# A scan-and-FFN kernel on one core: the second pair's output products before the third FFN step, the third pair's loads behind a mask

## The chip, the cores and the metric

The kernel runs on one core of one Trainium2 chip. A core has TensorE (PE in the profile), which multiplies matrices into PSUM; VectorE (DVE), ScalarE (ACT) and GpSimd (POOL) for element work; SyncE (SP), whose queue issues transfers; and 16 DMA engines. The metric is the device time of one execution, in microseconds (us); lower is better.

## The reference

A state-space scan runs over 4 batches of 8 heads, 768 positions, head width 32 and state width 16. Its output, 3072 tokens of width 256, goes through a feed-forward layer (FFN) with 2048 hidden units and a squared relu.

```python
for c in range(nc):                                  # chunks of 32 positions
    L = np.exp(cum[:, :, :, None] - cum[:, :, None, :]) * causal
    M = np.einsum('bhin,bhjn->bhij', Cc, Bc) * L
    y_intra = np.einsum('bhij,bhjd->bhid', M, xc)
    y_inter = np.einsum('bhin,bhnd->bhid', Cc, state) * decay_to_i[:, :, :, None]
    y[:, :, sl] = y_intra + y_inter
    Bx = np.einsum('bhjn,bhjd->bhjnd', Bc, xc) * decay_from_j[:, :, :, None, None]
    state = decay_full[:, :, None, None] * state + np.sum(Bx, axis=2)
x = attn_out.transpose(0, 2, 1, 3).reshape(B * S, H * D)
h = np.maximum(x @ w_in, 0.0)
out = h * h @ w_out
```

The result does not depend on the chunk length; the kernel uses chunks of 128 positions. All inputs and the output are float32 in memory.

## The kernel before

**Pairs.** The tokens are cut into 12 blocks of 256, one for each batch and third of the sequence, called pairs because each holds two chunks of 128 positions. Pair k has number k in the code, from 0: the "second pair" is k = 1, the "third" k = 2. The first four pairs are the first thirds of the four batches and need no earlier state.

**What one pair does.** Its C, B and x are loaded (`ph_load`, L122) into buffers of a pool of three. `prep_c`, `prep_b` and `prep_x` (L148, L164, L180) scale and cast them to bf16: cz, Bb and xs. `ph_tr` (L202) transposes Bb and cz on PE and copies them to bct. `ph_mt` (L220) multiplies them to the matrix M in PSUM, and `ph_mask` (L236) applies the causal mask on DVE, in four quarters q = 0 to 3, into mts. `ph_u` (L242) computes the chunk's contribution U to the state, and `ph_s` (L265) turns it into the state. `ph_y` (L324) computes the output: `y_intra` (L307) has 32 small products of mts and xs that go through the quarters in the order 0, 1, 2, 3, then 8 products with the state; ScalarE copies the sum to T in bf16 (L366).

**The FFN.** A pair's FFN has 8 steps. Step (pair, f) multiplies T with two of the 16 column tiles of w_in (`mm1`, L372, four products "hps"), applies relu on ScalarE into hb, squares on DVE (`square`, L384) and, four steps later, multiplies with two row tiles of w_out (`mm2`, L390, four products "ops"). The PSUM pool for hps has two buffers, so a step can begin only when the relu of the step two before it has read its buffer. `warm` (L473) issues dummy products ("dps").

**What sets the order.** The order of work on each engine is written out by hand (`tc.manual_schedule`, L450); waits between engines follow from the data. After a prologue for pair 0, a loop (L629) goes through the list `steps`: first four steps of pair 0, then four of pair 1, then the rest. At each s it issues `mm1`, then whatever `at(s, ...)` put into `todo`, then a square and an `mm2`. `ph_y(1)` is called at the top of s = 3, ahead of the fourth step's `mm1` and behind the third's. The masks of pair 1 come at s = 0 (q = 0, 1) and at s = 1 (q = 3, then q = 2, both from a bf16 copy mtc that ScalarE makes at s = 0).

**When loads start.** SP issues the loads in program order. With `gate=nc.gpsimd`, GpSimd first writes one element of each destination buffer, and the load waits for that write; so a load cannot start before GpSimd's queue has come to it. The weights are loaded from GpSimd's own queue, cast on the way: w_in in four parts (`load_wi`, L135) and w_out in four (`load_wo`, L140). `late_loads` (L568) holds the last three of them until T of pair 1 exists, by copying one element of it to `touch`. The load of pair 2 stands in the prologue (L552), ahead of w_in tiles 8 to 11 on GpSimd's queue.

Of the kernel before, what the change touches and what calls it, by code (L numbers as in the profile page):

```python
# [16 lines left out]
def _fap(base: bass.AP, offset_elems: int, free_dims):  # L17

    ap0 = list(base.ap)[0]
    return bass.AP(tensor=base.tensor, offset=base.offset + offset_elems,  # L20
                   ap=[list(ap0)] + [list(d) for d in free_dims])


def _dap(base: bass.AP, offset_elems: int, dims):

    return bass.AP(tensor=base.tensor, offset=base.offset + offset_elems,
                   ap=[list(d) for d in dims])
# [3 lines left out]
def kernel(  # L31
# [14 lines left out]
    nc = tc.nc  # L46
# [51 lines left out]
    touch = const.tile([128, 1], FP32, name="touch")  # L98
# [23 lines left out]
    def ph_load(k, order="CBx", eng=None, gate=None):  # L122
        b, j = PAIRS[k]
        t = loaded.setdefault(k, {})
        for what in order:
            src, w = {"B": (B, N), "C": (C, N), "x": (x, D)}[what]
            dst = nat.tile([128, NH, 2 * w], FP32, tag=f"{what}_nat", name=f"{what}_nat{k}")
            if gate is not None:
                gate.memset(dst[:, 0, 0:1], 0.0)
            (eng or nc.sync).dma_start(  # L130
                out=dst, in_=_dap(src, (b * NH * S + j * 256) * w,
                                  [[2 * w, 128], [S * w, NH], [1, 2 * w]]))
            t[what] = dst
# [12 lines left out]
    live = {}  # L146
# [225 lines left out]
    def mm1(blk, fp):  # L372
        hps = ps_h.tile([128, 2, 256], FP32, tag="hps", name=f"hps{blk}_{fp}")
        for i in range(2):
            f = 2 * fp + i
            for g in range(2):
                nc.tensor.matmul(hps[:, i, :], w_in_b[:, g, f * 128:(f + 1) * 128],  # L377
                                 T[blk][:, g].rearrange("p r u t -> p (r u t)"),
                                 start=(g == 0), stop=(g == 1), skip_group_check=True)
        hb = fpool.tile([128, 2, 256], BF16, tag="hb", name=f"hb{blk}_{fp}")  # L380
        nc.scalar.activation(out=hb, in_=hps, func=AF.Relu)  # L381
        hbs[(blk, fp)] = hb

    def square(blk, fp):  # L384
        hb = hbs.pop((blk, fp))
        h2 = hpool.tile([128, 2, 256], BF16, tag="h2", name=f"h2{blk}_{fp}")
        nc.vector.tensor_tensor(out=h2, in0=hb, in1=hb, op=ALU.mult)  # L387
        h2s[(blk, fp)] = h2

    def mm2(blk, fp):  # L390
        if fp == 0:
            t = ps_o.tile([128, 2, 256], FP32, tag="ops", name=f"ops{blk}")
            ops[blk] = [[t[:, 0, :]], [t[:, 1, :]]]
            if blk == NPAIR - 1:
                ops[blk][1] = [ps_s.tile([128, 128], FP32, tag="A", name=f"ops_r1{c}", padded_shape=[128, 1024])
                               for c in range(2)]
            else:
                ops_t[blk] = t
        h2 = h2s.pop((blk, fp))
        for i in range(2):  # L400
            f = 2 * fp + i
            for r in range(2):
                o = ops[blk][r]
                for c in range(len(o)):
                    nc.tensor.matmul(o[c], h2[:, i, r * 128:(r + 1) * 128],  # L405
                                     w_out_b[:, f, c * 128:(c + 1) * 128] if len(o) > 1 else w_out_b[:, f, :],
                                     start=(f == 0 and (r == 0 or blk == NPAIR - 1)), stop=(f == 15),
                                     skip_group_check=True)
        if fp == 7:
            finish_block(blk)  # L410
# [39 lines left out]
    with tc.manual_schedule():  # L450
# [17 lines left out]
        def idle_tile(pool=ps_o, tag="ops"):  # L468
            idle.append(pool.tile([128, 256], FP32, tag=tag, name=f"dps{len(idle)}", padded_shape=[128, 512]))
# [3 lines left out]
        def warm(n, cols=256):  # L473
            for _ in range(n):
                nc.tensor.matmul(idle[-1][:, 0:cols], dum[:, 0:128], dum[:, 0:cols],  # L475
                                 start=True, stop=True, skip_group_check=True)
# [13 lines left out]
        for r in range(2):  # L490
            nc.scalar.copy(out=_fap(C_r, r * 128, [[16, 2], [32, 4], [1, 16]]),
                           in_=_fap(loaded[0]["C"], r * 16, [[128, 2], [32, 4], [1, 16]]))
# [28 lines left out]
        def recip(b0, nb, j):  # L521

            nc.vector.reciprocal(out=_fap(Pinv, b0 * 24 + j, [[96, 2], [3, 8 * nb]]),
                                 in_=_fap(P_sb, b0 * 24 + j, [[96, 2], [3, 8 * nb]]))
# [24 lines left out]
        ph_y(0)  # L549
        ph_tr(1)  # L550
        recip(2, 2, 0)
        ph_load(2, gate=nc.gpsimd)  # L552
        idle_tile()
        warm(3, 128)

# [5 lines left out]
        def at(s, fn, *args):  # L561
            todo.setdefault(max(s, 0), []).append((fn, args))
# [9 lines left out]
            load_wo(12, 16)  # L572

        at(0, load_wi, 8, 12)
        at(3, own_decay)
        at(5, late_loads)
        at(6, lambda: ph_load(3, gate=nc.gpsimd))
# [49 lines left out]
            at(yy, ph_y, k)  # L627
        waiting = []
        for s in range(len(steps) + LAG):  # L629
            if s == 3:  # L630
                ph_y(1)
            if s < len(steps):
                mm1(*steps[s])
                waiting.append(steps[s])
            if 1 <= s < 3:
                warm(3, 128)
            if s == 4:
                waiting[2:4] = []
            if s == 6:
                waiting[2:2] = steps[2:4]  # L640
            for fn, args in todo.pop(s, []):
                fn(*args)
            if 1 <= s < len(steps) + 1:
                square(*steps[s - 1])
            if 4 <= s < len(steps):
                mm2(*waiting.pop(0))
# [31 lines left out]
```

## Time and profile before

| | |
|---|---|
| median of 13 runs | 119.5 us |
| lowest and highest | 118.05 and 123.81 us |
| the profiled execution's own time | 118.05 us |
| its span, first to last instruction | 116.3 us |
| granted TensorE clock | 1.000 |
| busy: PE, weight loads, DVE, ACT, POOL | 94%, 77%, 74%, 66%, 30% |
| moved by DMA | 13.63 MB, mean 117 GB/s |

The profile describes one execution. Its times are microseconds from the first instruction. "SPq" is SP's queue at the moment at which it issues a transfer; "PEld" is the loading of weights into TensorE, which overlaps with products. An entry in brackets at a line of the timeline is the idle time of that engine just before it, and what ended it. "issue" is time in which an engine waited for nothing that the profile shows. In the lists of transfers the last number is the time from issue to landing.

### The profile page before, as it was taken

How to read it: one execution, taken by the hardware profiler on the slowest of the kernel's cores; microseconds unless marked ns; L12 is line 12 of the kernel's file. 1: busy time of each engine (PE TensorE's matmuls, PEld its weight loads, DVE VectorE, ACT ScalarE, POOL GpSimd, SP SyncE). 2: the span in 40 equal slices, each digit the busy share in tenths (PEclk: the TensorE clock that was granted, in tenths of full speed). 3: DMA queues.
4: the chain of work that ended last, by engine and by line, in shares of the span. 5: the costliest groups of instructions: out<-in, count | busy, mean ns of one | idle time of the engine just before them, and what ended most of it. 6: DMA issues, size and time to landing. Idle time of an engine off the chain costs nothing.

```text
span 116.3 us, 4065 instructions
## 1 busy us (share of the span) xinstructions
PE 109.2 (94%) x1672; PEld 89.8 (77%) x1672; DVE 86.4 (74%) x204; ACT 76.3 (66%) x146; POOL 34.3 (30%) x69
## 2 busy tenths in 40 slices
PE   6798889999999999999999999999999999999970
PEld 4575568787787788887887887887887888898960
DVE  6588837699599898895996995986966958744530
ACT  4563877667777666677586675775865965777720
POOL 0099337305894440701333324304300000000000
PEclk9999999999999999999999999999999999999999
DMA  3999999998899908719729939979060020200203
GB/s 90 190 176 154 162 207 189 131 201 136 166 234 178 200 25 163 164 58 175 111 90 169 85 99 204 44 159 185 3 158 8 13 77 6 82 8 0 94 2 90
DMA packets 50019, 13.63 MB, mean 117 GB/s; under 512 B 44304, under 2 KB 49104, under 8 KB 50000
## 3 DMA queue, kind: packets, MB, share of 16 engines
q1 hardware_dynamic: 46400, 10.98, 53.4%
q0 software_dynamic: 3200, 2.10, 13.4%
q10 hardware_dynamic: 400, 0.28, 1.0%
q8 instruction: 13, 0.21, 0.8%
q14 instruction: 6, 0.05, 0.2%
HBM read 10.74 MB, written 3.15 MB: 119 GB/s over the span
## 4 chain that ended last, share of the span: by engine, by line
PE 78%; DMA 10%; DVE 4%; POOL 2%; ACT 1%; issue 1%; ACTq 0%; DVEq 0%; SPq 0%
PE ops L405 33%; PE hps L377 32%; DMA w_in_b<-in_moe_w_in_dram 5%; PE Y L314 3%; DMA C_nat<-in_C_dram 3%; PE mt L227 3%; DMA cf<-const_f 3%; DVE mts L238 2%; PE Y L343 2%; PE U L256 1%; POOL xs L183 1%; POOL bc L152 1%; PE ops_r L405 1%; PE ops L421 1%; PE ops_r L421 1%
## 5 line engine op out<-in xcount | busy, mean ns | idle before, releaser
L381 ACT ACTIVATE hb<-hps 128x512 bf16<-128x512 f32 x96 | 57.6, 600 | 29.9 <-PE hps L377 28.8
L377 PE MATMUL hps<-T,w_in_b 128*128 128x256 bf16 x384 | 57.6, 273 | 0.7 <-DVE bct L217 0.4
L405 PE MATMUL ops<-w_out_b,h 128*128 128x256 bf16 x360 | 55.0, 273 | 0.0
L387 DVE TENSOR_TENSOR h<-hb 128x512 bf16<-128x512 bf16 x96 | 41.9, 460 | 10.7 <-ACT hb L381 10.5
L377 PEld LDWEIGHTS <-w_in_b 128*128 128x128 bf16 x384 | 37.2, 98 | 5.4 <-DMA w_in_b<-in_moe_w_in_dram 0.8
L405 PEld LDWEIGHTS <-h 128*128 128x128 bf16 x376 | 34.5, 98 | 6.3 <-issue 2.0
L238 DVE TENSOR_TENSOR mts<-mt,cb 128x512 bf16<-128x512 f32 x44 | 29.0, 682 | 9.0 <-PE mt L227 9.0
L183 POOL TENSOR_TENSOR xs<-x_nat,Pinv 128x512 bf16<-128x512 f32 x12 | 13.5, 1123 | 12.1 <-DMA x_nat<-in_x_dram 8.5
L152 POOL TENSOR_TENSOR bc<-C_nat,P_sb 128x128 bf16<-128x128 f32 x16 | 6.6, 433 | 21.6 <-DMA C_nat<-in_C_dram 17.8
L475 PE MATMUL dps<-dum 128*128 128x128 bf16 (+1 forms) x58 | 6.8, 264 | 1.1 <-DVE dum L457 1.1
L300 DVE TENSOR_TENSOR S<-z,Pown 128x256 bf16<-128x256 f32 x16 | 7.3, 458 | 0.5
L366 ACT CAST T<-Y 128x512 bf16<-128x512 f32 x11 | 6.4, 585 | 0.5 <-PE Y L347 0.5
L443 ACT COPY osb<-ops 128x512 f32<-128x512 f32 x11 | 6.4, 581 | 0.2 <-PE ops L405 0.2
L475 PEld LDWEIGHTS <-dum 128*128 128x128 bf16 x58 | 4.6, 110 | 2.3 <-DVE dum L457 1.1
L314 PE MATMUL Y<-mts,xs 64*32 64x128 bf16 x384 | 5.2, 219 | 0.2 <-issue 0.2
L227 PE MATMUL mt<-bct 32*64 32x256 bf16 x192 | 5.1, 280 | 0.2 <-DVE bct L515 0.2
L177 POOL CAST bc<-B_nat 128x128 bf16<-128x128 f32 x16 | 5.2, 350 | 0.4 <-DMA B_nat<-in_B_dram 0.4
L314 PEld LDWEIGHTS <-xs 64*32 64x32 bf16 x384 | 3.0, 91 | 1.8 <-issue 0.7
L227 PEld LDWEIGHTS <-bct 32*64 32x64 bf16 x192 | 1.9, 102 | 2.7 <-issue 1.7
L293 DVE SCALAR_TENSOR_TENSOR z<-z,Ptot,U 128x64 f32<-128x64 f32 x12 | 3.2, 266 | 0.4 <-PE U L256 0.3
L141 POOL DMA_DIRECT2D w_out_b<-in_moe_w_out_dram x4 | 3.1, 780 | 0.3 <-issue 0.3
L217 DVE COPY bct<-tr 128x768 bf16<-128x768 bf16 x3 | 1.7, 556 | 2.0 <-PE tr L210 2.0
(72 smaller groups left out, 54.9 us busy)
## 6 DMA issues: line engine op xcount, KB each, us to landing
x_nat<-in_x_dram SPq DMA_DIRECT2D x12, 256.0 KB, 4.4
out_dram<-osb SPq DMA_DIRECT2D x7, 256.0 KB, 2.4
C_nat<-in_C_dram SPq DMA_DIRECT2D x12, 128.0 KB, 3.4
B_nat<-in_B_dram SPq DMA_DIRECT2D x12, 128.0 KB, 3.7
w_in_b<-in_moe_w_in_dram POOLq DMA_DIRECT2D x4, 256.0 KB, 6.0
w_out_b<-in_moe_w_out_dram POOLq DMA_DIRECT2D x4, 256.0 KB, 6.8
out_dram<-osb SPq DMA_DIRECT2D x8, 128.0 KB, 1.8
bct<-bc SPq DMA_TRANSPOSE x8, 4.7
```

Of the source, the lines that this page charges most:

```text
L152: eng.tensor_tensor(out=_fap(bc[k % 3], r * 384 + 128, [[144, 2], [32, 4], [1, 16]]), in0=_fap(loaded[k]["C"], r * 16, [[128, 2], [32, 4], ...
L183: eng.tensor_tensor(out=_fap(xs, 0, [[256, 2], [32, 8], [1, 32]]), in0=_fap(loaded[k]["x"], 0, [[32, 2], [64, 8], [1, 32]]), in1=_fap(Pinv ...
L227: nc.tensor.matmul(mt[q // 2][64 * u:64 * u + 64, q % 2, r, :, :], bct[32 * q:32 * q + 32, r, 0, u * 64:u * 64 + 64], _fap(bct[32 * q:32 * ...
L238: nc.vector.tensor_tensor(out=v["mts"][:, q], in0=v["mt"][q // 2][:, q % 2] if src is None else src, in1=_fap(cb, 128, [[128, 2], [0, 2], ...
L300: nc.vector.tensor_tensor(out=S_n.rearrange("p (g q d) -> p g q d", g=2, q=4), in0=_fap(z, 0, [[32, 2], [0, 4], [1, 32]]), in1=_fap(Pown, ...
L314: nc.tensor.matmul(Y[u][32 * q:32 * q + 32, g, :], v["xs"][64 * u:64 * u + 64, r, h * 32:h * 32 + 32], v["mts"][64 * u:64 * u + 64, q, r, ...
L366: nc.scalar.copy(out=_fap(T[k], 0, [[64, 2], [128, 4], [1, 64]]), in_=_fap(Y[0], 0, [[512, 2], [64, 4], [1, 64]]))
L377: nc.tensor.matmul(hps[:, i, :], w_in_b[:, g, f * 128:(f + 1) * 128], T[blk][:, g].rearrange("p r u t -> p (r u t)"), start=(g == 0), stop ...
L381: nc.scalar.activation(out=hb, in_=hps, func=AF.Relu)
L387: nc.vector.tensor_tensor(out=h2, in0=hb, in1=hb, op=ALU.mult)
L405: nc.tensor.matmul(o[c], h2[:, i, r * 128:(r + 1) * 128], w_out_b[:, f, c * 128:(c + 1) * 128] if len(o) > 1 else w_out_b[:, f, :], start= ...
L475: nc.tensor.matmul(idle[-1][:, 0:cols], dum[:, 0:128], dum[:, 0:cols], start=True, stop=True, skip_group_check=True)
```

## The change

Two things are moved. `ph_y(1)`, the output products of the second pair, is called at s = 2 instead of s = 3, so it stands ahead of the third FFN step's products on PE, and its copy to T ahead of that step's relu on ScalarE. And the third pair's loads leave the prologue: at s = 2 GpSimd first copies one element of quarter 2 of the second pair's masked matrix to `touch`, and only then writes the gates of the three loads. On GpSimd's queue they now stand behind the load of w_in tiles 8 to 11.

```diff
@@ prologue
         ph_y(0)
         ph_tr(1)
         recip(2, 2, 0)
-        ph_load(2, gate=nc.gpsimd)
         idle_tile()
         warm(3, 128)
@@ schedule
         at(0, load_wi, 8, 12)
+
+        def third_loads():
+            nc.gpsimd.tensor_copy(out=touch, in_=live[1]["mts"][:, 2, 0, 0, 0:1])
+            ph_load(2, gate=nc.gpsimd)
+
+        at(2, third_loads)
         at(3, own_decay)
@@ loop
         for s in range(len(steps) + LAG):
-            if s == 3:
+            if s == 2:
                 ph_y(1)
             if s < len(steps):
                 mm1(*steps[s])
```

The number of products and of bytes is the same; GpSimd has one more instruction, the copy to `touch`.

## The prediction

> **What bounds the kernel now.** I read the page's fourth part first (the chain of work that ended last), then that chain in order of time from 12 to 17 us, then the timeline of all engines there, then the transfers.
>
> ```profile
> PE 78%; DMA 10%; DVE 4%; POOL 2%; ACT 1%; issue 1%; ACTq 0%; DVEq 0%; SPq 0%
> ```
>
> TensorE (PE) carries 78% of the chain. The shares do not say where it can be shortened; the order of time does. Columns are start, length, work:
>
> ```profile
> 8.00 5.60 DMA w_in_b<-in_moe_w_in_dram
> 13.60 0.05 issue
> 13.64 0.61 PE hps L377 x4
> 14.25 0.17 PE dps L475 x3
> 14.42 0.34 PE Y L314 x29
> 14.76 0.15 issue
> 14.91 0.23 PE Y L314 x3
> 15.14 0.25 PE Y L347 x8
> 15.39 0.02 issue
> 15.41 0.59 ACT T L366
> 16.01 0.04 issue
> 16.05 0.60 PE hps L377 x4
> ```
>
> Until 16.05 us the start-up is a chain of waits: w_in tiles 4 to 7 land at 13.60, the third FFN step runs, then the second pair's output products (Y), then ScalarE's copy into T, and at 16.05 the fifth step, the first to read that T. From 16.05 on, PE hardly stops: the windows view has it busy 8.55 of the 8.55 us to 24.60. So a shift of the 16.05 goes to the end one for one, and so does any new hole. The change works exactly before this point.
>
> The timeline has what else must be ready (start, length, engine, line, work):
>
> ```profile
> 13.22 0.75 DVE L238 TENSOR_TENSOR mts<-mtc,cb 128x512 bf16<-128x512 bf16 x2
> 13.26 0.25 PE L256 MATMUL U<-xs,Bb 64*32 64x64 bf16 x16 [0.42 <-ACT mtc L587]
> 13.62 0.31 ACT L279 ACTIVATE Sf<-U,Ptot 128x64 bf16<-128x64 f32 x1
> 26.64 0.42 PE L314 MATMUL Y<-mts,xs 64*32 64x128 bf16 x32
> 27.33 0.58 ACT L366 CAST T<-Y 128x512 bf16<-128x512 f32 x1
> ```
>
> The pair's four masks are done at 13.22 + 0.75 = 13.97, its state (Sf) at 13.93. The last two lines are the same product block one pair later: 0.69 from its first product to its T copy.
>
> **Part 1: Y ahead of the third step.** No arithmetic is added or removed: four hps products and three dummy ones change places with 40 Y products; on ScalarE the T copy goes ahead of the third step's relu. What was serial (landing, hps, Y) now overlaps with the masks, so Y starts earlier, yet not at PE's 13.51 (end of U): the third product needs mask slot 2, which the code masks last, at 13.97. Release to start costs 0.06 (T ends 15.99, hps starts 16.05), so Y runs from 14.03 and T could begin at 14.03 + 0.69 = 14.72 and end at 15.30, 0.69 earlier than 15.99.
>
> Most of that is not gained. The fifth step also needs a free hps buffer, and that is freed by the third step's relu, which now stands behind T on ScalarE. The third step follows the state products by 0.22 (15.07 to 15.29 in the trace), so it runs from 14.03 + 0.35 + 0.22 = 14.60 to 15.21; its relu (0.60, row "hb<-hps") goes from 15.25, overlapping T's tail by 0.05 as it does now, to 15.85; the fifth step starts at 15.90. Gain: **0.15 us**. The landing at 13.60 is then off the path, covered until 14.60; with that cover gone it would again be 13.64 plus the block.
>
> The 0.15 of "issue" at 14.76 decides the sign. It is PE's only wait of that name in this kernel: 29 products leave, the 30th does not until 14.91, and nothing is waited for. The page's third part has a queue for instructions (13 packets, 0.21 MB), and one such packet lies in the window 11.42 to 14.0. The Trainium skill (Runtime: NRT & Kernel Launch, "Instruction fetch mechanics") says that engines stream their code in 16 KiB blocks and that this is hidden by the issue rate. By that rule the hole is no fetch and the gain of 0.15 stands. The row differs: a hole with no releaser just after a fetch. I take the row. A fetch asked for before the change acts arrives at the same absolute time, so PE cannot pass that place in its stream before 14.91. In the new order the place (430 rows in) is the fifth of the eight state products. They then end at 15.15, T runs 15.17 to 15.75, the third step 15.13 to 15.74, its relu 15.70 to 16.30, and the fifth step starts at about 16.35: **0.30 us later** than now. So the bounds of this part are -0.15 and +0.30; I take +0.30.
>
> **Part 2: the third pair's loads wait for the mask.** On POOL one touch (0.19, the L569 row) and three memsets (0.14 each) move behind the w_in 8-11 load and wait for 13.97. That load's issue comes 0.1 earlier. Queued behind them on POOL: Pown (0.36), needed first at 19.86, and the touch of T with the three late weight loads; T ends at 15.30 to 15.75 instead of 15.99, so these loads start 0.25 to 0.7 earlier. On SP everything behind follows: C of the third pair is issued at 14.5 instead of 11.42, B at 15.0 instead of 11.89, x at 15.9 instead of 12.84.
>
> What does a delay of 3.1 us do? The transfers issued at those times took (issue to landing):
>
> ```profile
> C_nat<-in_C_dram SPq DMA_DIRECT2D x1, 128.0 KB, 7.3
> B_nat<-in_B_dram SPq DMA_DIRECT2D x1, 128.0 KB, 7.3
> x_nat<-in_x_dram SPq DMA_DIRECT2D x1, 256.0 KB, 8.2
> ```
>
> So C lands at 18.7, B at 19.2, x at 21.06. The readers: ScalarE copies B at 20.67 (slack 1.5), in front of its next relu; the transposes at 21.0 need C's product on POOL (0.67), slack 1.6; the U products at 24.61 need xs (1.06 on POOL, begun at 21.19), slack 24.61 - 1.06 - 0.1 - 21.06 = 2.4.
>
> Here the Trainium skill speaks against the change: DMA: Bandwidth & Descriptors, "Queues, rings and completion order", says that each DMA engine takes its queues in turn. If so, the loads were served from their issue on, and 3.1 us of delay is 3.1 us of lateness: B 1.6 over its slack, x 0.7 over. The sum would be about 1.6 + 0.3, some 121.4. The row, the transfers of 11.42 to 14.0, says otherwise:
>
> ```profile
> DMA packets 692, 0.39 MB, mean 153 GB/s; under 512 B 27, under 2 KB 691, under 8 KB 691
> q0 software_dynamic: 691, 0.38, 117.4%
> q8 instruction: 1, 0.02, 3.3%
> ```
>
> All data here is the software queue's, the weights; the hardware queue with C moved nothing for 2.6 us after its issue. From 14.0 to 16.5 it got 906 packets beside 610. So the old issue bought only a place from 14.0 on. In the new order the engines go on with w_out 4-7 and w_in 8-11 (256 KB each; by the packet records one such load took 1.76 us when alone) to about 16.7, and C starts at 14.5 plus 1.8 to 2.6 (the second pair's and this delay), 16.3 to 17.1. The work is the same and the engines stay busy, so little is lost. C and B, 2048 packets, took 4.6 us beside weights and, by the packet records, 2.0 alone for the second pair; I take 2.7: B lands at about 19.9 with the 0.5 from last packet to landing, inside its 20.67 by 0.8. x follows, now against late weights that start sooner; before, x landed 7.0 after C's first packet, in new order 5 to 7: 21.3 to 24.1. I take 22.7, inside the 23.4 by 0.7. So the part costs **0**, with bounds 0 and 1.6. If the cover goes, ScalarE's copy holds the relu, then PE, and x's lateness holds U and all behind it, one for one.
>
> **Sum.** The profiled execution took 118.05: span 116.3 and 1.75 around it. 116.3 + 0.30 + 0 + 1.75 = 118.35. The median shown is 1.45 above this execution, so against 119.5 I predict **119.8**. 0.5% is 0.6 us, about what a measurement of this kernel tells from no change.
>
> **Rivals.** (a) The fetch is hidden or moves: fifth step at 15.90, 119.35. For it: the rule, and that a fetch is seen only as a packet. Against: no other releaser for the hole. Still no change by the bound. (b) *Third pair too late*: the loads land after their readers; one mechanism, at the B copy or at U. It decides when B lands after 20.7 or x after 23.5. For it: slacks of 0.7 to 0.8 after my estimate, against an uncertainty of a microsecond; the fourth pair's C, issued at 19.01, moved nothing until 22.6. Against: engines without a hole. An x at 24.4 gives U at 25.6, +1.0, with the 0.3 +1.3: 120.8. (c) *Faster*: T is ready 0.7 earlier and the late weights with it; if the buffer release is not what holds the fifth step and the fetch does not either, it starts at 15.35, 0.7 earlier: 118.8. Against: the relu's place behind T in the written order. (d) The change does not do what it says: Y really waits for slot 2 until 13.97 anyway, so the reordering buys an idle half microsecond; that is inside my sum.
>
> **How the numbers follow.** My forecast with (a) 0.45, all within 0.5%; (b) 0.39, of which nearly all is slower; (c) 0.16. Faster 0.16, same 0.45, slower 0.39. The range: 118.4 holds most of (c) with the spread of medians, 121.4 most of (b). The likeliest case's own range is 119.3 to 120.0.
>
> **What would show it.** Right: first Y product waits for DVE's mask and runs near 14.0; a hole of PE among L347 ending near 14.9; the fifth step at 16.2 to 16.4; C of the third pair issued near 14.5 and no wait in front of the B copy or U. Wrong: the hole gone and the fifth step at 15.9 (a); ScalarE idle before L175 until a landing, or PE idle before L256 until POOL's xs (b); a fifth step before 15.6 (c).

## The result and the profile after

The changed kernel takes 121.2 us (median of 11 runs, 119.88 to 123.53), the kernel before 120.3 us in the runs beside it (median of 48, 118.04 to 123.9). The ratio is 1.0151, 95% interval 1.0111 to 1.0192: about 1.8 us slower. Executions of one kernel spread over some 5 us here, so the ratio is taken over undisturbed ones only (the lowest times are 1.84 apart, the medians of all 0.9), and the mechanism is read from single profiles.

The profiled execution took 119.88 us with a span of 118.0 (before: 118.05 and 116.3). Shares of its chain by engine:

```profile
PE 77%; DMA 15%; DVE 3%; POOL 1%; issue 1%; ACT 0%; DVEq 0%; POOLq 0%
```

The share of DMA rose from 10% to 15%. The chain in order of time says where (start, length, work):

```profile
13.50 0.41 PE Y L314 x30
13.91 0.16 PE Y L347 x4
14.07 0.20 issue
14.27 0.26 PE Y L347 x4
14.53 0.02 issue
14.55 0.41 ACT T L366
14.97 10.23 DMA x_nat<-in_x_dram
25.20 0.03 issue
25.22 0.02 POOLq L183
25.24 0.09 issue
25.33 1.07 POOL xs L183
26.40 0.04 issue
26.44 0.26 PE U L256 x16
```

The third pair's x is issued at 14.97 and lands at 25.20; POOL turns it into xs, and only then can PE form U. Before, x was issued at 12.84, landed at 21.06, and U at 24.61 waited for nothing; the line between is the first of the late weight loads:

```profile
12.84 3.54 SPq L130 DMA_DIRECT2D x_nat<-in_x_dram  x1
16.59 0.81 POOL L141 DMA_DIRECT2D w_out_b<-in_moe_w_out_dram  x1 [0.27 <-issue]
24.61 0.25 PE L256 MATMUL U<-xs,Bb 64*32 64x64 bf16 x16
```

After, PE's list of waits (who waited for what, us in total, times, longest) has the new entry:

```profile
PE U L256 <- POOL xs L183: 2.1, 1, 2.1
```

I count from the start of the first FFN step (10.99 before, 10.48 after), since the executions start differently. The fifth step starts 5.06 later before and 5.25 after, +0.19. The 13th stands at +0.20. Between it and the 14th U stalls: the 14th is +2.34, and the last step of the kernel +2.22. Nothing of this is given back. With the first step 0.51 earlier in this execution, 2.22 - 0.51 is the 1.7 between the spans.

Why a transfer issued 2.1 later lands 4.1 later is to be seen in the transfers of 19.1 to 20.6 (queue: packets, MB, share of 16 engines):

```profile
DMA packets 321, 0.24 MB, mean 161 GB/s; under 512 B 19, under 2 KB 321, under 8 KB 321
q0 software_dynamic: 319, 0.24, 114.7%
q1 hardware_dynamic: 2, 0.00, 0.2%
```

The engines are full, almost with late weights from the software queue alone (q0, the loads that GpSimd issues; q1 has those of SP). C and B ended at 19.03, and x, issued at 14.97, has its first packet, known by its 256 bytes, only at 20.56. The late weight loads were issued just after x:

```profile
14.97 2.74 SPq L130 DMA_DIRECT2D x_nat<-in_x_dram  x1
15.27 0.18 POOL L568 CAST touch<-T 128x1 f32<-128x1 bf16 x1 [0.95 <-ACT T L366]
15.72 0.81 POOL L141 DMA_DIRECT2D w_out_b<-in_moe_w_out_dram  x1 [0.27 <-issue]
```

x's lead over them is 0.75 us. Before it was 3.75: x at 12.84, the first late weight load at 16.59. The lead shrank from both sides, but not equally: counted from the first step, x goes 2.64 later because of the mask, and the weights go 0.36 earlier because T is ready earlier.

### The profile page after: what moved, and what is told of

Read it like the earlier page. It is cut to its first block, busy times and chain, and to the rows that moved or that the text cites. A ratio compares the mean times of both kernels' runs of the same rounds, so it can differ in the third digit from the quotient of the medians.

```text
span 118.0 us, 4067 instructions
## 1 busy us (share of the span) xinstructions
PE 109.2 (93%) x1672; PEld 90.0 (76%) x1672; DVE 86.2 (73%) x204; ACT 76.4 (65%) x146; POOL 34.3 (29%) x70
## 2 busy tenths in 40 slices
DMA packets 50019, 13.63 MB, mean 116 GB/s; under 512 B 44304, under 2 KB 49104, under 8 KB 50000
## 4 chain that ended last, share of the span: by engine, by line
PE 77%; DMA 15%; DVE 3%; POOL 1%; issue 1%; ACT 0%; DVEq 0%; POOLq 0%
PE ops L405 32%; PE hps L377 31%; DMA x_nat<-in_x_dram 9%; DMA w_in_b<-in_moe_w_in_dram 4%; PE Y L314 3%; PE mt L227 3%; DMA a_nat<-in_a_dram 2%; DVE mts L238 2%; PE Y L343 2%; PE U L256 1%; POOL xs L183 1%; PE ops_r L405 1%; PE ops L421 1%; PE Y L347 1%; PE ops_r L421 1%
## 5 line engine op out<-in xcount | busy, mean ns | idle before, releaser
L256 PE MATMUL U<-xs,Bb 64*32 64x64 bf16 x64 | 1.0, 195 | 2.5 <-POOL xs L183 2.1
```

## The experiments

Each expectation was written before its run and names the theories as they stood then. The one that the runs led to is this: x is late because the late weight loads get in front of it. Its rivals are that the delay of x alone does it whatever the weights do, that the hole among the products costs the time, and that the landing merely scatters between executions. Where the executions gave no interval, this is said.

### One half at a time

Products only: the kernel before with

```diff
-            if s == 3:
+            if s == 2:
                 ph_y(1)
```

> Only the second pair's products move ahead of the third step; the third pair's loads stay in the prologue. Theory A (the loss is the third pair's x, which lands after its reader because its loads were held back): no wait of PE before U of the third pair, x lands 8 to 9 us after its issue near 12.3, the fifth step starts 5.2 to 5.3 us after the first (5.06 in the kernel before, 5.25 in the changed one), with the hole of PE among the L347 products; ratio 1.002 (1.000 to 1.004). Rival R1 (the new order of products and relu carries half of the loss or more): ratio 1.007 or above.

> The products alone once more, with more executions, since four were too few for an interval. Theory A (x after its reader): no wait of PE for POOL's xs; ratio 1.002 (0.998 to 1.006). R1 (the new order carries the loss): 1.007 or above. Theory F, after the first looks: PE stops at the same place of its instruction stream (matmul 221) until a fetch of instructions has landed, 1.45 to 1.6 us after its packet ends; the products ahead reach that place earlier and wait longer, but end at the same time: the hole's end is again 1.4 to 1.7 us after the end of the first fetch packet.

The first group of executions gave 118.62 to 124.78 us in 4 runs and no interval; in its profile U waits 0.7 for a mask of DVE, which the last section takes up. The second gave a ratio of 1.0051 (1.0002 to 1.0100). In its profile x lands 7.8 after an issue at 12.76, with a lead of 3.84, and no wait for xs appears in PE's list. Of the eight entries there, these two belong to the moved products:

```profile
PE Y L347 <- issue: 0.5, 1, 0.5
PE Y L314 <- DVE mts L238: 0.4, 1, 0.4
```

So this half alone gives the hole among the state products, not the late x. It is no gain; it costs a third of the 1.5% by its middle value, and up to two thirds by its interval.

Loads only: the move of `third_loads` with `ph_y(1)` left at s = 3.

```diff
-        ph_load(2, gate=nc.gpsimd)
...
+        def third_loads():
+            nc.gpsimd.tensor_copy(out=touch, in_=live[1]["mts"][:, 2, 0, 0, 0:1])
+            ph_load(2, gate=nc.gpsimd)
+
+        at(2, third_loads)
```

> Only the third pair's loads wait for the mask; the products stay behind the third step. Theory A: x lands 10 us after its issue near 15, PE waits 1.5 to 2.5 us before U of the third pair for POOL's xs; ratio 1.013 (1.009 to 1.018). R1: no more than half of the loss, ratio 1.007 or below.

> The loads alone once more. Theory A, as first put: ratio 1.013 (1.009 to 1.018), PE waits before U of the third pair for xs by 1.5 to 2.5 us. Theory A2 (x is late only where the late weight loads get in front of it; they are released by T, and T is about 0.7 us earlier only with the products ahead): x is served before the late w_out tiles, no wait before U, ratio 1.002 (0.997 to 1.007).

> The loads alone, a third execution; in the two before there was no wait before U, but a late fetch (1.6 us) in one and late w_in tiles 4 to 7 (1.5 us) in the other. A2 with chance: where the start is not held up, T exists near 16 and the late weights move near 18.2, about with x: a wait before U of 0 to 2 us. L: again a hold before the fifth step of 1 us or more, none before U.

> The loads alone, once more, for an execution whose start is not late. A2: T near 16, late weights from 18, x in competition with them: x lands 7 to 10 us after its issue near 15, PE waits 0 to 2 us before U; ratio 1.010 (1.003 to 1.018). Rival L: no wait before U in an early start either, and ratio below 1.004.

The first gave 118.31 to 120.5 us in 4 runs, without an interval; the second 1.0147 (1.0056 to 1.0237, six runs); the third, a single one, 122.69; the last 1.0064 (1.0014 to 1.0114, 20 runs). The first three profiles caught executions whose first step starts between 11.7 and 12.1 us. They lost time by a hole among the Y products (1.6), by a wait for w_in (1.5), and by both (1.3 and 1.0), and none shows a wait for xs. The fourth starts at 11.1, as the kernels before and after did:

```profile
15.62 2.04 SPq L130 DMA_DIRECT2D x_nat<-in_x_dram  x1
16.39 0.81 POOL L141 DMA_DIRECT2D w_out_b<-in_moe_w_out_dram  x1 [0.27 <-issue]
23.63 1.06 POOL L183 TENSOR_TENSOR xs<-x_nat,Pinv 128x512 bf16<-128x512 f32 x1 [3.84 <-DMA x_nat<-in_x_dram]
24.75 0.25 PE L256 MATMUL U<-xs,Bb 64*32 64x64 bf16 x16 [0.30 <-POOL xs L183]
```

The same delay of x, with the same lead of 0.77, but x lands 7.9 after its issue and U waits 0.3. So the loads alone put x at the edge; they do not account for a wait of 2.1. The two ratios of this one kernel are far apart but their intervals overlap; by the narrower one the halves sum to 1.0115, by the other to 1.0198, with the whole at 1.0151. What share each half has in the time is therefore not settled by the times.

### Take the mask's wait away, or only bring it forward

The changed kernel without the line that touches mts, so the loads wait only for their turn in POOL's queue:

```diff
         def third_loads():
-            nc.gpsimd.tensor_copy(out=touch, in_=live[1]["mts"][:, 2, 0, 0, 0:1])
             ph_load(2, gate=nc.gpsimd)
```

> The changed kernel without the touch of the mask: the third pair's loads stand behind the load of w_in tiles 8 to 11 on POOL, but wait for nothing else. Theory A: C issued near 11.2, x lands before 22, no wait before U; ratio 1.002 (1.000 to 1.004). Rival R2 (the place behind the w_in load makes x late, not the wait for the mask): x lands after 24 and PE waits before U by 1.5 us or more; ratio 1.010 or above.

The ratio to before is 0.9985 (0.9931 to 1.0040, 20 runs): the loss is gone, with both moves in place and the hole still there (`PE Y L347`, 0.6). x and the late weights in its timeline:

```profile
13.79 3.35 SPq L130 DMA_DIRECT2D x_nat<-in_x_dram  x1
16.24 0.81 POOL L141 DMA_DIRECT2D w_out_b<-in_moe_w_out_dram  x1 [0.27 <-issue]
22.84 1.09 POOL L183 TENSOR_TENSOR xs<-x_nat,Pinv 128x512 bf16<-128x512 f32 x1 [2.67 <-DVE h L387]
24.96 0.26 PE L256 MATMUL U<-xs,Bb 64*32 64x64 bf16 x16
```

The lead is 2.45, x lands 8.9 after its issue, xs no longer waits for it last, and U waits for nothing. So the wait for the mask, not the new place of the loads in the queue, is what costs.

A half dose, touching quarter 0 (masked first) in place of quarter 2:

```diff
-            nc.gpsimd.tensor_copy(out=touch, in_=live[1]["mts"][:, 2, 0, 0, 0:1])
+            nc.gpsimd.tensor_copy(out=touch, in_=live[1]["mts"][:, 0, 0, 0, 0:1])
```

> The changed kernel with the loads released by mask slot 0 instead of 2: the release comes 1.3 us earlier (slot 0 ends 1.28 us before slot 2). Theory A with a threshold (x is served in time if it is queued before the late w_out tiles 8 to 11 begin to move, near 17.3): x lands before 22.5, no wait before U; ratio 1.002 (1.000 to 1.004). Theory A in proportion (every us of delay costs about as much): x lands near 23, PE waits 0 to 0.5 us; ratio 1.002 to 1.007. R2: as before, 1.010 or above.

Inconclusive: 121.37 to 124.49 us in 4 runs, no interval. Its profile starts late (first step 11.95), with a hole of 0.9, a granted clock of 0.5 from 16.1 to 19.5, x landing 6.2 after its issue at 15.54, and no wait for xs.

### Change the weights instead of x

The changed kernel, with the late weights held for the second pair's first relu in place of T:

```diff
-            nc.gpsimd.tensor_copy(out=touch, in_=T[1][:, 0, 0, 0, 0:1])
+            nc.gpsimd.tensor_copy(out=touch, in_=hbs[(1, 0)][:, 0, 0:1])
```

> The changed kernel with the three late weight loads released by the fifth step's relu instead of the second pair's T, some 1.8 us later. A2: x begins to move before or with the late w_out tiles, lands at 21 to 23, PE waits at most 0.5 us before U; ratio 1.003 (0.998 to 1.008), unless the sixth quarter's w_in tiles are now late (a wait before the step that reads them, up to 1 us). Theory A without A2 (x is late by its own later issue): x lands at 24.5 or later, PE waits 1.5 us or more before U; ratio 1.012 or above.

This tells the late weights from the delay alone: x is issued as late as in the changed kernel, and only the weights move. The timeline of this kernel:

```profile
14.93 2.46 SPq L130 DMA_DIRECT2D x_nat<-in_x_dram  x1
17.59 0.81 POOL L141 DMA_DIRECT2D w_out_b<-in_moe_w_out_dram  x1
21.30 1.06 POOL L183 TENSOR_TENSOR xs<-x_nat,Pinv 128x512 bf16<-128x512 f32 x1 [0.53 <-DMA x_nat<-in_x_dram]
24.84 0.61 PE L377 MATMUL hps<-T,w_in_b 128*128 128x256 bf16 x4 [0.91 <-DMA w_in_b<-in_moe_w_in_dram]
25.38 0.25 PE L256 MATMUL U<-xs,Bb 64*32 64x64 bf16 x16
```

Issued at the same moment, x lands after 6.2 us, not 10.2, and PE's wait before U is gone. The engines are then late with the other side: PE waits 0.9 for w_in. Part of the stall has moved: 0.9 in place of 2.1. It took 118.92 us in the profiled execution and 122.69 to 123.15 in the other three, without an interval, so it is no remedy that can be claimed.

The other way, the changed kernel with two of the late weight loads left out (w_in and w_out tiles 12 to 15 are never loaded, the products use tiles 0 to 3 in their place):

```diff
             load_wo(8, 12)
-            load_wi(12, 16)
-            load_wo(12, 16)
```

> The changed kernel without its two last weight loads (w_in and w_out tiles 12 to 15 are left out, and tiles 0 to 3 stand in for them in the products). If x is late by standing behind the late weights, of which only w_out 8 to 11 is left: x begins when that has moved, near 19, lands at 21 to 22.5, PE waits 0 to 0.5 us before U. If x is late by its own later issue whatever else moves: lands at 24.5 or later, a wait of 1.5 us or more.

One execution, 121.7 us, and again a late start (12.22, hole 0.9). x is issued at 16.71 and lands 7.3 later, its packets running from 20.6 to 23.38, behind the start of w_out tiles 8 to 11 at 19.75. That x still comes behind the one late load that is left agrees with the theory, but the late start had given x its slack back, so it decides little.

### Is it there in every execution?

The changed kernel itself, profiled twice more:

> The changed kernel itself, another execution: is the late x the rule? Theory A2: x begins to move only after the late w_out tiles (more than 1 us after their first packet), lands 9.5 us or more after its issue, PE waits 1 to 2.5 us before U of the third pair. Rival L (luck: the late x was one execution's; the loss of the others is a later start or a longer fetch hole): no wait before U, the loss stands before the fifth step.

> The changed kernel, a third execution. A2: as in the second, a wait of 1 to 2.5 us before U. L: none; the fifth step comes 6 us or more after the first, or the first step after 11.5.

They took 124.36 and 120.89 us. The second starts early, at 10.69, as the first profile did:

```profile
15.27 3.31 SPq L130 DMA_DIRECT2D x_nat<-in_x_dram  x1
16.28 0.81 POOL L141 DMA_DIRECT2D w_out_b<-in_moe_w_out_dram  x1 [0.27 <-issue]
26.21 1.06 POOL L183 TENSOR_TENSOR xs<-x_nat,Pinv 128x512 bf16<-128x512 f32 x1 [5.63 <-DMA x_nat<-in_x_dram]
27.32 0.25 PE L256 MATMUL U<-xs,Bb 64*32 64x64 bf16 x16 [0.86 <-POOL xs L183]
```

The late x is repeated: lead 1.0, landing after 10.8. The other execution starts at 12.26 and has a different loss, a hole of 2.2 among the state products. T is then late, the late weights go at 19.56, x at 17.06 leads them by 2.5, lands after 5.4 and nobody waits for it. So each of the three profiled executions of the changed kernel lost either by the late x or, with a late start, by a long hole. The clock took its share in two of them: it was 0.5 from 15.0 to 18.4 in the one that starts early, and from 16.9 to 23.7 in the late one. In the former the fifth step comes 6.31 after the first, not 5.25, and PE comes to U 15.8 after it, not 13.8, so the wait of 0.9 shows only a part of x's delay.

Is that long hole the change's? The kernel before, unaltered, twice more:

> The kernel before itself, another execution, to see what its holes are. Theory A2 with F: no wait of PE for POOL's xs before U whatever the start; where the clock comes up late (first step after 11.5) the hole at matmul 221 is 1 us or more here too, so that this loss is not the change's. Rival H (the held-back loads make the fetch later): a late start, if it comes, with a hole below 0.8 us.

> The kernel before, a third execution. As in the second: no wait for xs before U; a hole of 1 us or more only with a late start.

120.76 and 119.08 us, and both start late (12.37 and 12.15). The first has

```profile
17.58 0.23 PE L314 MATMUL Y<-mts,xs 64*32 64x128 bf16 x3 [1.34 <-issue]
```

at the place where the first profile of before had 0.15; the second has no hole at all. So the long hole is not the change's own; how often each kernel has it, these few profiles do not tell. In neither does U wait for xs; x lands after 7.7 and 7.5.

### The hole by itself

If the hole is PE waiting for its next block of instructions, a shorter stream of instructions ahead of it should move it in the work and not in the stream. The kernel before, with half as many dummy products of twice the width (256 columns, the same lasting time) in the prologue:

```diff
-        warm(14, 128)
+        warm(7)
...
-        warm(8, 128)
+        warm(4)
...
-            warm(6, 128)
+            warm(3)
```

> The kernel before with 28 dummy products of 128 columns replaced by 14 of 256: the same busy time of PE, 28 instruction rows fewer. Theory F: the place at which the fetch is waited for moves 28 rows later in the work, behind the second pair's products; no hole within L314 or L347, the fifth step starts 4.6 to 4.9 us after the first instead of 5.06; where the fetch lands late the fifth step waits for it. Ratio 0.996 (0.990 to 1.000). Rival (the hole is tied to the products' shape or to their operands): a hole within L314 or L347 as before, ratio 0.998 to 1.003.

The products of the second pair then run without a break:

```profile
14.65 0.42 PE L314 MATMUL Y<-mts,xs 64*32 64x128 bf16 x32
15.00 0.29 PE L347 MATMUL Y<-bct,Sf 32*32 32x128 bf16 x8
```

and the fifth step stands at +4.81 in place of +5.06. The ratio is 0.9966 (0.9928 to 1.0004, 22 runs): nearly a gain, but the interval takes in no change. Going on with five more blocks of dummies:

> The kernel before with all 43 dummy products of 128 columns after the first batch replaced by 26 wider ones at nearly the same busy time: the 28 rows fewer of the earlier run and some 10 more. F: the place of the fetch lies behind the fifth step's products; where the fetch lands late, less of its lateness counts; the dummies cost 0.1 us more. Ratio 0.996 (0.991 to 1.000). Rival: the place alone doesn't matter once it is out of Y: no better than 0.9966 and worse by the dummies, 0.998 or above.

1.0027 (0.9981 to 1.0073), fifth step at +4.94: no more is to be had there, and the 0.9966 is not confirmed by this neighbour.

The same edit beneath the products' move, and beneath the whole change:

> Products ahead of the third step, loads as before, and the 28 dummy products replaced by 14 wider ones. F: no hole in the products (the place lies 28 rows later, behind the third step); the fifth step 4.8 to 5.0 after the first; ratio 0.997 (0.992 to 1.001), as with the shorter stream alone or 0.1 us better. Rival: the earlier T releases the late weights before x and gives the gain back: ratio 1.000 or above, a wait before U.

> The changed kernel with the same 14 wider dummy products, which takes the hole out of the products. A2: T is early in every execution, so the late weights get in front of x: x lands 9.5 us or more after its issue, PE waits 1 to 2.5 us before U; ratio 1.010 (1.006 to 1.016) to the kernel before. Rival H (the loss is mainly the fetch hole): ratio 1.003 or below, no wait before U.

Products first with the shorter stream: 1.0033 (0.9984 to 1.0081). Its profile starts late (12.09). The hole has gone behind the products,

```profile
17.61 0.70 PE L377 MATMUL hps<-T,w_in_b 128*128 128x256 bf16 x5 [0.83 <-issue]
```

at the same count of PE's products. The whole change with the shorter stream: 1.0182 (1.0088 to 1.0276, 4 runs), so a T freed from its hole does not help the change. The order in the engines is worse; the timeline:

```profile
15.12 3.28 SPq L130 DMA_DIRECT2D x_nat<-in_x_dram  x1
15.49 0.81 POOL L141 DMA_DIRECT2D w_out_b<-in_moe_w_out_dram  x1 [0.27 <-issue]
26.37 1.06 POOL L183 TENSOR_TENSOR xs<-x_nat,Pinv 128x512 bf16<-128x512 f32 x1 [5.90 <-DMA x_nat<-in_x_dram]
```

The lead is 0.37, the landing takes 11.1, U waits 1.8, and this time B is late as well (`PE tr L208` waits 1.0 for ScalarE's copy). With x's issue almost where the changed kernel has it (14.97) and the weights 0.23 sooner, a second load went past its reader.

### Lead and landing together

In the executions that start early (x's lead is from the start of its issue to that of the first late weight load's):

| kernel | lead, us | x: issue to landing, us | U waits for xs, us |
|---|---|---|---|
| before | 3.75 | 8.2 | 0 |
| before, shorter stream | 3.79 | 8.4 | 0 |
| before, shorter still | 3.85 | 7.9 | 0 |
| products only (second) | 3.84 | 7.8 | 0 |
| products only (first) | 3.5 | 9.5 | 0 |
| no mask wait | 2.45 | 8.9 | 0 |
| late weights later | 2.66 | 6.2 | 0 |
| loads only (fourth) | 0.77 | 7.9 | 0.3 |
| changed | 0.75 | 10.2 | 2.1 |
| changed, third profile | 1.0 | 10.8 | 0.9 |
| changed, shorter stream | 0.37 | 11.1 | 1.8 |

Every wait for xs stands at a lead of 1.0 or less, none at 2.45 or more. But the lead does not fix the landing: it took 7.9 at 0.77 in the loads-only row and 9.5 at 3.5, and with a late start, the products first and the shorter stream even 10.8 at 3.93.

The end of SP's issue sorts the landings better than its start. SP is busy with x's issue for 1.7 to 4.5 us (2.74 in the changed kernel, to 17.71). In the twelve profiles, of all twenty, in which it is through before the first late weight load or at most 0.05 after its start, x lands 5.1 to 8.4 after its issue. In the eight in which it is not, x takes 7.3 (with two of the late loads left out) and 7.9 to 11.1. Late starts are among both. This was seen in the profiles and not tested by a run.

## Why the prediction was wrong

The prediction was 119.8 us, no change. It came out as its rival (b), *Third pair too late*, which it had put at 0.39 and at 120.8.

**Bound.** Right: what moved the start-up went to the end one for one. The +2.34 at the 14th step is +2.22 at the last.

**Part 1, Y ahead of the third step: right in mechanism, a little off in size.** The hole did fall on "the fifth of the eight state products": four run, 0.20 of issue, four more. Taking the row was right: by the word of the Trainium skill (Runtime: NRT & Kernel Launch, "Instruction fetch mechanics") that fetching is hidden, the prediction had the hole as no fetch and a gain of 0.15, and the hole was there again, 0.20 us of it. The term +0.30 was mis-sized and measured +0.19 at the fifth step. One reason can be read off: the hole ended at 14.27, not at 14.91. Its end was not bound to an absolute time as the step assumed; it came 0.64 sooner where the first step came 0.51 sooner. Rival (c) did not occur, nor did (a): the hole is still there.

**Part 2, third pair's loads wait for the mask: this is the step that failed.** The text took 0 for it, "the work is the same and the engines stay busy, so little is lost". Its first links held or were cautious: C was issued at 13.88 (forecast 14.5), x at 14.97 (15.9), and C's first packet was at 15.50, 1.6 after its issue (16.3 to 17.1 from 1.8 to 2.6; the second pair's 1.8 reads 2.0 in the trace). The break is in the next link, the time from C's first packet to x's landing, "in new order 5 to 7". It measured 25.20 - 15.50 = 9.7. C and B were through at 19.03, 3.5 after their start (2.7 was taken) and still sooner than forecast. Then the hardware queue got 2 packets in 1.5 us and x began at 20.56. It landed at 25.20 against the limit of 23.5 that rival (b) named, 1.7 too late, and PE waited 2.1. The engines did stay busy, as argued, but with what nobody needed yet.

The text had named the cause in passing ("now against late weights that start sooner"; they "start 0.25 to 0.7 earlier") and counted it into the width of the range only. The runs put it first. Let x go sooner by taking the mask's wait away, and the kernel is level with before, 0.9985: that the wait for the mask makes the loss is shown by the times. Leave x as late as it is and let the weights go later, and x is on time: so the delay of x alone does not make the wait, the late weights have a part in it. This second step rests on one profile, not on times. The products' move adds to it where T comes sooner, since it is T that releases the weights: T ended at 15.13, 4.65 after the first step, and at 15.99, 5.00 after it, before. The fourth execution with the loads alone, which has no hole, had its T 4.70 after the first step and the same lead without that move. So a sum of +0.30 and 0 leaves out what the first part can do to the second, but that it did so in the median is not shown.

Of the rule of the Trainium skill (DMA: Bandwidth & Descriptors, "Queues, rings and completion order") that a DMA engine takes in turn the queues for which it has work, the prediction said that it would give 1.6 + 0.3 and 121.4. That is near the measured size, but by luck: there the 1.6 was B's lateness, while here nobody waited for B, and x was 1.7 late, not 0.7. The trace has x unserved from its issue to 20.56, at the end with 319 packets to 2. That goes against the rule only if x's packets stood ready by then, which no view shows.

**What stays open.** Why the hardware queue gets nothing for so long is argued from counts of packets only; whether it is the arbitration or a latency at the start of a transfer was not told apart. The share of the loads' half in the time is open (1.0147 and 1.0064). The products-only kernel's 1.0051 was not taken apart. Why the loads-only kernel's x landed after 7.9 and the changed kernel's after 10.2, with the same lead, is open.

A late start goes with a slow TensorE in the prologue: its 14 dummy products take 0.95 us in the first profile of before and 1.67 in the second, and the record of the granted clock begins, at full clock, at 4.2 and at 10.1. The other profiles divide alike: 4.0 to 4.7 with an early start, 8.7 to 10.1 with a late one, except that one late start has a clock of 0.5 from 7.3 to 10.7. What decides it is open. So is whether the change has a part in the clock's later drops: the mean clock was below 0.99 in 8 of 14 executions of the changed kernel and in 38 of 131 of the kernel before.

## What to carry to other kernels

When a change frees one thing earlier and holds another back, list all transfers that each release starts and put them in one order by issue. Here the engines were busy either way, and what cost time was whose data they moved. Keep a lead ahead of a bulk load that nobody needs yet: here no reader of x waited with 2.45 us or more, and four profiles with 1.0 or less had a wait. Or hold the bulk load for something later, and then watch its own reader (0.9 here). And read two or three executions before you trust a profile's hole: it was 0, 0.15 and 1.3 us in three profiles of one kernel.

## What the hardware showed that was not expected

**A hole at a fixed place in the stream.** In before and in the changed kernel alike, the hole stands at the same count of PE's matmuls (after 221 of them): ahead of the 30th Y product in one, of the fifth state product in the other. With dummies merged it moved in the work and kept its count. In the fifteen profiles that have it, it ends 1.39 to 1.57 us after the end of the first packet of 16 KiB on the instruction queue: 13.42 to 14.91 before, 12.79 to 14.27 after, 16.08 to 17.58 in the second profile of before, 14.42 to 15.90 in the changed kernel with the shorter stream. Its length went from 0.15 to 2.2 us, depending on how far PE had come by then. The third profile of before has none; there that packet ended at 13.63, and PE came to the place at 15.49, 1.86 later. That the hole is an instruction fetch fits all of these and was not shown otherwise.

**A queue served alone.** With transfers issued on both, the engines moved 691 packets of the software queue and none of the hardware queue's for 2.6 us before the change, and 319 to 2 for 1.5 us after it. In the changed kernel with the shorter stream, 19.5 to 21.5:

```profile
q0 software_dynamic: 371, 0.27, 109.6%
q1 hardware_dynamic: 63, 0.01, 3.8%
```

**VectorE beside GpSimd.** The DVE product S, 128x256 f32, takes 0.41 to 0.43 us where no product or copy of POOL runs beside it. Where one of POOL's had begun first and overlaps it by 0.18 or more, S takes the time of the overlap and some 0.28 more: 0.86 with 0.58, 0.98 with 0.70, 1.28 with 1.00, as if it stood still until POOL was through. Where S began first, it takes 0.41 to 0.43 beside up to 0.41 of POOL's work. This holds in all twenty profiles; the kernel before has a 0.98 at 60.72. In the kernel with the products first and the shorter stream:

```profile
23.99 1.17 POOL L183 TENSOR_TENSOR xs<-x_nat,Pinv 128x512 bf16<-128x512 f32 x1 [3.48 <-DVE bct L217]
24.16 1.29 DVE L300 TENSOR_TENSOR S<-z,Pown 128x256 bf16<-128x256 f32 x1
```

Here and in the first profile of the products alone (1.28 at 22.29) the masks stand behind such an S on DVE, and U then waited 0.7 for a mask. No run took POOL's xs away to test it.
